# A spectral filter and a two-level expert layer on one core: a block-diagonal table for the forward transform, PSUM units whose two banks are no longer ordered, a third store buffer and a new written order

## The chip, the cores and the metric

The kernel runs on one core of one Trainium2 chip. The metric is the device time of one execution in microseconds, the median over several runs. The core has five engines that run side by side and meet at semaphores: TensorE (PE for its matmuls, PEld for its weight loads), VectorE (DVE), ScalarE (ACT), GpSimd (POOL) and SyncE (SP, which here only issues DMAs). Matmuls write PSUM, which has eight banks of 128 x 512 fp32; ACT and DVE read it.

## What is computed

x is 8 x 1856 x 256 in fp32. The first part is a filter over the 1856 positions of each of the eight sequences:

```
X  = rfft(x, axis=1)
Yr = Xr @ w_r - Xi @ w_i + b_r
Yi = Xr @ w_i + Xi @ w_r + b_i
Y  = soft_threshold(Yr, 0.01) + 1j * soft_threshold(Yi, 0.01)
y  = irfft(Y, n=1856, axis=1)
```

The second part sends each of the 14848 rows of y to one of 4 groups and, inside it, to one of 4 experts, by the largest of two sets of logits. The expert computes relu(row @ w1) @ w2 with 1024 hidden values, scaled by the two softmax weights of the choice. An expert's rows are known only when the rows before it have been routed.

## The kernel before

**Two parts.** The span falls into a part whose order is written out by hand (about its first 565 us) and a part that works through all experts (the rest). In the second part line 455 is the first matmul of an expert (up), lines 516 and 517 the second (down). The diff does not touch it. The first part does the transforms, the routing and some early expert work, so that TensorE has something to do while routing ends.

**The steps of the first part.** The sequences go through in four pairs. One letter of the string ORDER is one step, and PE, ACT, DVE and SP each execute their instructions in that order. POOL's queue is filled by the framework's scheduler, but a scatter is tied to the matmul of two PE steps before it. The letters:

- l: a load of x or of an expert's weights (SP). c, d: first stage of the forward transform, 64 x 64 matmuls (line 324, PE), then transposes into the tile zys (line 328, DVE).
- e: second stage, with the table T (line 584, PE). One e makes two frequencies k. f and h: ACT copies the result of one k as its high half (line 597), DVE subtracts to get the low half (line 602).
- j, k, n, m, o: ACT writes the bias into PSUM (line 607), PE does twelve 128 x 512 matmuls for the complex weights (line 616), ACT takes the positive and the negative relu (line 624, tiles rp and rn, two buffers each), DVE subtracts them into zys (line 630).
- r, s: first stage back (line 644, PE; transposes at line 652, DVE). v: second stage back (line 663, PE). w and x: ACT copies one half of the v result to a store buffer ysb (line 674; two buffers) and after both halves issues the store to ys_d (line 676); DVE transposes the same half into yt (line 682; five buffers).
- G, H, R, S: logits by 64 matmul instructions on four yt tiles (line 692), a transpose (line 701), some 33 small steps of routing for a half pair (lines 156 to 231, DVE and a little ACT and PE), and the scatter of one column of row numbers into the lists (line 240, POOL).
- W, V, I, Z, F, T, X, Y, U, A, B, D, E, J, K: early expert work for eight jobs: split of the weights into halves, lists, fetch of rows (line 422, POOL), transposes (line 762), the up matmuls (line 783), the relu and its low half (lines 791, 795), the down matmuls (lines 807, 809), the scaling (line 817, ACT), the sum (line 823, DVE) and the store (line 502, POOL). L and M read the final lists and fetch the first rows of the second part.

**PSUM in the first part.** The pool "pa" holds three units of two banks (`banks()`); c, e, r, v, G, the routing matmuls, T and D each take one, and a step that needs a fourth waits until the oldest has been read. Two more banks hold the k results. The framework orders every two accesses to one unit that come from different engines, in the order in which they are written. In e one k lies in 256 columns of both banks; in v and D the halves lie one in each bank.

**fp32.** An fp32 matmul of the source shows up in the trace as two loads and two matmul instructions (480 matmuls of e are 960 of line 584). The matmuls of e take 64 rows: zys keeps one sequence of the pair in partitions 0 to 63 and the other in 64 to 127, and T holds the same 64 x 64 table twice, one below the other, so that a matmul per half is issued.

Of the kernel before, what the change touches and what calls it, by code (L numbers as in the profile page):

```python
# [9 lines left out]
F32 = mybir.dt.float32  # L10
# [27 lines left out]
jejleffhlhkknmjofhcmncdjdfkddhokmnjocmncdjedddocffchhkddddkmnjocmncdjedddoeffhhkkmnjofhemfnhkjoefmhnejokkmfnhjokmfnhjokm  # L38
njofhemnjokfhkmfnhjokfnhmjormnjokssrmnjoesseffhhkrfmhnkjssorfmhnkjssovnmvxwxvwxwvxwxvjxkxxwwxowwGnmjowwvxHvwxwvxxcwRxwxc
xwdlwRdGRddRRRRRRcHcdcdldcddledddefRfRhhcRRcddklddRRRRkRfRRmhnRRRjRkfmhnojoRknmjoRenRmRRjReRffhRRSRkhRoRRSRRRRkRfRnSRmRh  # L40
joRkRfSRmhnRRRjRSRRkRmRRnSjooRRneRmSRefRRjRSReRfohhSkSkfnhSmjorSmfnhkjsSsSormfnhSkjssSormSnjoesSskfhSrmSfnhcjsSscSdvldvx
wwdSkxwwxxSdovmSnvxwxvwxwvSxwxGjoSwwwSwkxxxSHRvmRRSnvxwxcwxcwSxwdlGjdSddRRRRRcRReddRReHRffhhkRRRRRRRRRRkRmfonhjoRkmnjofR
hemRnRjRkRfRRhSRRRoRkmRSRfRRnRRhjSRkmRRnojoSRRReRmRRnRSRRjRReRffcShdlkhSdoRkmSfnhjoSRkmRnRRSjRRRcmRoSncdjdldSdoeSrffhShk
ssSrmSnjoksSsSrmnjoeSssefSfhhkSSrfmhnSkjssSovfnShvwxwvxwxvSwxmvxxjSkxwxwxwoSwvmnGSjowwSwwkHSxxxRSRvRnRRvwxwxexwwxIRGmRRf
RfRjRRhRZhkHRRRRRRRRkRmRRnjooRRneRmRjRReRffRhSRRkRhRSRRRSRRRRknRRfoRmRSRRjRRefhSmhnRRSRkRjRRooSRkfmShnSjoRkfRmRnRRjSRRem
hSnRokjoSfhkmSnoSmSnorFsSsrWSWVWVSWTsWWFsWWVrXVSYlVUSsUsSABrAVBVSUWsWSWsUWSAVvAVlBvwxwvxSwxvwxSxvxSxWxWxWBWVwSVwVGwSVwlV
# [72 lines left out]
def spectral_moe(ctx: ExitStack, tc: tile.TileContext, x, wri, bri, wgate, w1, w2, cst, out):  # L119
# [171 lines left out]
    T = cf.tile([128, K1, 64], F32, name="T")  # L291
# [885 lines left out]
```

## Time and profile before

| | |
|---|---|
| median of 3 runs | 1218.77 us (1211.72 to 1220.06) |
| profiled execution | 1220.21 us, of which the span from first to last instruction is 1218.4 us |
| PE busy | 1139.5 us, 94% |
| DVE, ACT, POOL busy | 664.1, 540.9 and 397.0 us |
| mean granted TensorE clock | 0.967 |
| instructions | 20694 |

The busy time of PE is a union of modelled matmul intervals, so two matmuls that overlap count once, and a busy PE is not PE at its peak. An idle time stands in brackets behind an instruction with the instruction that ended it. The granted clock is 1.0 or 0.5 at any moment; a figure between is a mean over a stretch.

### The profile page before, as it was taken

To read this page: it belongs to the slowest core of one execution; us is meant where nothing else is said; L and a number is where in the kernel's file an instruction comes from. 1 tells how busy PE (TensorE), PEld (TensorE's weight loads), DVE (VectorE), ACT (ScalarE), POOL (GpSimd) and SP (SyncE) were. 2 spreads that over 40 slices of the span, in tenths; PEclk is the share of its full clock that TensorE was granted. 3 is DMA by queue.
4 is the path that set the end of the run, shared out by engine and by line. 5 is a ranking of instruction groups with operands and counts; after the bars stand their busy time and mean duration, and the time that the engine had idled before them with its cause. 6 is when DMAs were issued, how large, how long until landed. Compare 5 with 4: busy or idle time off the path is not lost. (4 is left out here: it accounts for less than half of the span.)

```text
span 1218.4 us, 20694 instructions
## 1 busy us (share of the span) xinstructions
PE 1139.5 (94%) x7762; PEld 913.8 (75%) x7762; DVE 664.1 (55%) x1453; ACT 540.9 (44%) x1234; POOL 397.0 (33%) x450
## 2 busy tenths in 40 slices
PE   8999899799898767998999999999999999999996
PEld 5686586476675456887889888888888898788886
DVE  3535774676575745634565557346346564474452
ACT  2464364344445332422454446346345454363442
POOL 0000034314326334654233332332343333323321
PEclk8999999999899888998999999999999999999999
DMA  9400610412221543122143324434533354345300
GB/s 388 132 2 3 240 36 2 158 52 71 70 71 18 136 160 87 49 69 88 49 181 107 118 103 173 185 112 140 215 126 110 114 181 178 117 146 203 117 30 24
DMA packets 42360, 138.94 MB, mean 114 GB/s; under 512 B 17318, under 2 KB 19628, under 8 KB 31890
## 3 DMA queue, kind: packets, MB, share of 16 engines
q1 hardware_dynamic: 21458, 89.21, 21.2%
q0 software_dynamic: 15904, 31.48, 8.1%
q10 hardware_dynamic: 4896, 16.91, 3.7%
q8 instruction: 62, 1.02, 0.4%
q14 instruction: 40, 0.33, 0.1%
HBM read 103.49 MB, written 35.00 MB: 114 GB/s over the span
## 5 line engine op out<-in xcount | busy, mean ns | idle before, releaser
L516 PE MATMUL py<-big,hh 128*128 128x512 f32 x824 | 298.4, 402 | 0.0
L455 PE MATMUL ph<-xth,big 128*128 128x384 f32 (+1 forms) x896 | 257.8, 363 | 5.2 <-ACT xth L442 3.6
L240 POOL DMA_INDIRECT lst<-ent,sloti x128 | 132.2, 1033 | 335.7 <-DVE xl L602 189.6
L517 PE MATMUL py<-big,hl 128*128 128x256 f32 x824 | 231.6, 281 | 0.0
L461 DVE SCALAR_TENSOR_TENSOR hl<-ph,hh 128x256 fp32r<-128x256 f32 x448 | 151.0, 379 | 78.8 <-ACT hh L459 68.7
L455 PEld LDWEIGHTS ph<-xth,big 128*128 128x128 f32 x896 | 166.4, 189 | 25.1 <-ACT xth L442 3.8
L516 PEld LDWEIGHTS py<-big,hh 128*128 128x128 f32 x824 | 155.0, 188 | 37.4 <-issue 3.2
L459 ACT ACTIVATE hh<-ph 128x256 fp32r<-128x256 f32 x448 | 137.8, 371 | 85.2 <-PE ph L455 80.4
L455 PE MATMUL ph<-xtl,big 128*128 128x384 f32 (+1 forms) x448 | 162.4, 362 | 0.1
L502 POOL DMA_INDIRECT out_dram<-yo,si_f x96 | 97.7, 1018 | 183.7 <-DVE yo L524 159.3
L517 PEld LDWEIGHTS py<-big,hl 128*128 128x128 f32 x824 | 155.0, 188 | 0.1
L422 POOL DMA_INDIRECT xg<-ys_d,gi_f x96 | 93.5, 974 | 187.8 <-PE pg L438 164.1
L524 DVE SCALAR_TENSOR_TENSOR yo<-py,ent_f,yo 128x256 f32<-128x256 f32 x96 | 46.4, 483 | 163.3 <-ACT yo L523 122.5
L523 ACT ACTIVATE yo<-py,ent_f 128x256 f32<-128x256 f32 x96 | 45.6, 475 | 193.7 <-PE py L517 152.2
L405 DVE TENSOR_TENSOR big<-xt,big 128x512 fp32r<-128x512 f32 x160 | 108.8, 680 | 0.0
L404 ACT CAST big<-xt 128x512 fp32r<-128x512 f32 x160 | 104.0, 650 | 0.0
L616 PE MATMUL pw<-wh,xh 128*128 128x512 f32 x240 | 102.0, 425 | 0.0
L616 PE MATMUL pw<-wl,xh 128*128 128x512 f32 x240 | 97.6, 407 | 0.0
L455 PEld LDWEIGHTS ph<-xtl,big 128*128 128x128 f32 x448 | 84.9, 190 | 8.1 <-DVE xtl L443 0.5
L584 PEld LDWEIGHTS bank<-T,big 64*128 64x128 f32 x960 | 63.1, 205 | 15.7 <-issue 7.6
L584 PE MATMUL bank<-T,big 64*128 64x64 f32 x960 | 66.4, 293 | 4.6 <-DVE big L328 3.0
L624 ACT ACTIVATE rp<-pw,nlam 128x512 f32<-128x512 f32 x60 | 41.2, 687 | 65.7 <-PE pw L616 54.5
(187 smaller groups left out, 1629.1 us busy)
## 6 DMA issues: line engine op xcount, KB each, us to landing
xt<-in_w_dram SPq DMA_DIRECT2D x48, 1024.0 KB
ys_d<-ysb ACTq DMA_DIRECT2D x32, 512.0 KB
big<-in_w_dram SPq DMA_DIRECT2D x16, 1024.0 KB
big<-in_x_dram SPq DMA_DIRECT2D x8, 1024.0 KB
xt<-in_x_dram SPq DMA_DIRECT2D x8, 1024.0 KB
lst<-ent,sloti POOLq DMA_INDIRECT x128
lst<-zero SPq DMA_DIRECT2D x1, 1920.0 KB
xg<-ys_d,gi_f POOLq DMA_INDIRECT x96
```

What stands on the lines that cost most here:

```text
L240: ins = nc.gpsimd.indirect_dma_start(out=lst, out_offset=bass.IndirectOffsetOnAxis(ap=sl_, axis=0), in_=en_, in_offset=None, bounds_check= ...
L404: nc.scalar.copy(out=wt[:, 2 * i, cs], in_=raws[i][:, cs])
L405: nc.vector.tensor_tensor(out=wt[:, 2 * i + 1, cs], in0=raws[i][:, cs], in1=wt[:, 2 * i, cs].bitcast(F32), op=ALU.subtract)
L422: ins = nc.gpsimd.indirect_dma_start(out=xg[:, c, :], out_offset=None, in_=ys_d[0:rows, :], in_offset=bass.IndirectOffsetOnAxis(ap=ids.gi[ ...
L455: nc.tensor.matmul(o[:, :n], lhsT=a_[:, ch, fs], rhs=b_[:, ch, 0:n], start=k == 0, stop=k == 5)
L459: nc.scalar.activation(out=hh[:, f, :m], in_=ov, func=AF.Relu)
L461: nc.vector.scalar_tensor_tensor(out=hl[:, f, :m], in0=ov, scalar=0.0, in1=hh[:, f, :m].bitcast(F32), op0=ALU.max, op1=ALU.subtract)
L502: ins = nc.gpsimd.indirect_dma_start(out=out, out_offset=bass.IndirectOffsetOnAxis(ap=ids.si[:, t:t + 1], axis=0), in_=ysb, in_offset=None ...
L516: nc.tensor.matmul(o, lhsT=hh[:, f, ts], rhs=w2b[:, :, f, :], start=f == 0, stop=f == 7, skip_group_check=True)
L517: nc.tensor.matmul(o[:, 0:D], lhsT=hl[:, f, ts], rhs=w2h[:, f, :], start=False, stop=f == 7, skip_group_check=True)
L584: nc.tensor.matmul(ov, lhsT=zys[pr][rows_, k, bt, :, kp], rhs=T[rows_, 2 * k + kp, :], start=True, stop=True, skip_group_check=True)
L616: ins = nc.tensor.matmul(y, lhsT=a_[:, c * 128:c * 128 + 128], rhs=w_[:, c // 2, c % 2].rearrange("p j e -> p (j e)"), start=False, stop=a ...
```

## The change

- **The table.** T gets 128 columns per slot in place of 64 and is zeroed by POOL at the start. The raw table is loaded into a buffer of the pool "xt" (two buffers, which the loads of x and of weights use too), and POOL copies it into the two diagonal blocks, in three calls of two copies. A matmul of e then takes all 128 rows and writes 128 columns; the number of matmuls halves (240 in the source), and one k fills one bank in the order in which f and h want it.
- **Banks not ordered.** `apart` declares that f of one k and h of the other k of a unit, w of one half and x of the other half, and D of one half against E and J of the other have no dependency. w now takes the second half first while x takes the first.
- **Buffers.** ysb has three buffers (two before), yt four (five), rn one (two); rp has none, because the positive relu is written straight into zys and o subtracts rn there.
- **The order.** ORDER is another permutation of the same 1434 letters, each as often as before.

```diff
--- before.py
+++ after.py
...
@@ -288,7 +288,8 @@
     nc.scalar.dma_start(out=cA, in_=cst[:, _OFF["A"][0]:_OFF["A"][0] + 64])
     nc.scalar.dma_start(out=K, in_=cst[:, CK0:CK1])
     nc.vector.tensor_copy(out=base, in_=kc("EB"))
-    T = cf.tile([128, K1, 64], F32, name="T")
+    T = cf.tile([128, K1, 128], F32, name="T")
+    nc.gpsimd.memset(T, 0.0)
     wf = fwd.enter_context(tc.tile_pool(name="wf", bufs=2))
     pw = fwd.enter_context(tc.tile_pool(name="pw", bufs=2, space=PSUM))
 
@@ -344,8 +345,14 @@
         for bt in range(2):
             a_last = turn_a(0, i, bt, o[:, bt])
 
-    nc.sync.dma_start(out=T.rearrange("p k c -> p (k c)"), in_=cst[:, 0:CF1])
-    craw = wf.tile([128, 2 * D], F32, name="rn")[:, 0:128]
+    traw = xp.tile([128, K1, 64], F32, name="xt")
+    nc.sync.dma_start(out=traw.rearrange("p k c -> p (k c)"), in_=cst[:, 0:CF1])
+    def t_blocks(k):
+        for h in range(2):
+            nc.gpsimd.tensor_copy(out=T[64 * h:64 * h + 64, k].rearrange("p k (j h c) -> p k j h c", j=2, h=2)[:, :, :, h, :], in_=traw[64 * h:64 * h + 64, k, :].rearrange("p k (j c) -> p k j c", j=2))
+
+    t_blocks(slice(0, 6))
+    craw = wf.tile([128, 2 * D], F32, name="rn", bufs=1)[:, 0:128]
     nc.sync.dma_start(out=craw, in_=cst[:, CF1:CI0])
 
     wraw = xp.tile([128, 2, 2, D], F32, name="xt")
@@ -362,6 +369,8 @@
     for w_ in (wh, wl):
         nc.scalar.activation(out=w_[:, 1, :, 0], in_=w_[:, 0, :, 1].bitcast(F32), func=AF.Copy, scale=-1.0)
         nc.scalar.copy(out=w_[:, 1, :, 1], in_=w_[:, 0, :, 0].bitcast(F32))
+    t_blocks(slice(6, 18))
+    t_blocks(slice(18, 30))
     nc.scalar.copy(out=sl, in_=craw)
     nlam = cf.tile([128, 1], F32, name="nlam")
     nc.vector.memset(nlam, -LAM)
@@ -544,6 +553,11 @@
             return run()
         return wrap
 
+    def apart(ins, key, *others):
+        for o in others:
+            tc.declare_no_dep(ins.ins, group=str(o), reason="the two work in different banks")
+        tc.add_to_no_dep_group(str(key), ins.ins)
+
     def pop(key):
         return units.pop(key), low.pop(key)
 
@@ -573,33 +587,26 @@
 
     @steps_of(pairs, u8)
     def f_mm(pr, kk):
-        psum["f", pr, kk] = o = banks()
+        unit = banks()
         for k in range(2 * kk, min(2 * kk + 2, 15)):
+            psum["f", pr, k] = o = unit[:, k % 2]
             for kp in range(2):
                 for bt in range(2):
-                    c0 = k % 2 * 256 + (2 * kp + bt) * 32
-                    for h in range(2):
-                        rows_ = slice(64 * h, 64 * h + 64)
-                        ov = o[:, h, c0:c0 + 160].rearrange("p (j c) -> p j c", c=32)[:, 0:5:4]
-                        nc.tensor.matmul(ov, lhsT=zys[pr][rows_, k, bt, :, kp], rhs=T[rows_, 2 * k + kp, :], start=True, stop=True,
-                                         skip_group_check=True)
-
-    def f_view(pr, k):
-        o = psum["f", pr, k // 2][:, :, k % 2 * 256:k % 2 * 256 + 256]
-        return o.rearrange("p h (j c) -> p j h c", j=2)
-
-    def f_cols(t):
-        return t.rearrange("p (j h c) -> p j h c", j=2, h=2)
+                    m = 2 * kp + bt
+                    nc.tensor.matmul(o.rearrange("p (j c) -> p j c", j=4)[:, :, m * 32:m * 32 + 32],
+                                     lhsT=zys[pr][:, k, bt, :, kp], rhs=T[:, 2 * k + kp, :], start=True, stop=True,
+                                     skip_group_check=True)
 
     @steps_of(pairs, k15)
     def f_high(pr, k):
         units["f", pr, k] = xh = wf.tile([128, 512], F32R, name="xh")
-        nc.scalar.copy(out=f_cols(xh), in_=f_view(pr, k))
+        apart(nc.scalar.copy(out=xh, in_=psum["f", pr, k]), ("f", pr, k), ("h", pr, k ^ 1))
 
     @steps_of(pairs, k15)
     def f_low(pr, k):
         low["f", pr, k] = xl = wf.tile([128, 512], F32R, name="xl")
-        nc.vector.tensor_tensor(out=f_cols(xl), in0=f_view(pr, k), in1=f_cols(units["f", pr, k]).bitcast(F32), op=ALU.subtract)
+        apart(nc.vector.tensor_tensor(out=xl, in0=psum["f", pr, k], in1=units["f", pr, k].bitcast(F32), op=ALU.subtract),
+              ("h", pr, k), ("f", pr, k ^ 1))
 
     @steps_of(pairs, k15)
     def m_bias(pr, k):
@@ -609,6 +616,7 @@
     @steps_of(pairs, k15)
     def m_mm(pr, k):
         xh, xl = pop(("f", pr, k))
+        del psum["f", pr, k]
         y = psum["m", pr, k]
         for a_, ws in ((xh, (wh, wl)), (xl, (wh,))):
             for c in range(4):
@@ -620,14 +628,16 @@
     def m_relu(nm, store, sign):
         @steps_of(pairs, k15)
         def run(pr, k):
-            store[nm, pr, k] = t = wf.tile([128, 512], F32, name=nm)
+            t = z_of(pr)[:, k]
+            if sign < 0:
+                store[nm, pr, k] = t = wf.tile([128, 512], F32, name=nm, bufs=1)
             nc.scalar.activation(out=t, in_=psum["m", pr, k], func=AF.Relu, bias=nlam, scale=sign)
         return run
 
     @steps_of(pairs, k15)
     def m_sub(pr, k):
-        rp, rn = units.pop(("rp", pr, k)), low.pop(("rn", pr, k))
-        nc.vector.tensor_tensor(out=z_of(pr)[:, k], in0=rp, in1=rn, op=ALU.subtract)
+        z = z_of(pr)[:, k]
+        nc.vector.tensor_tensor(out=z, in0=z, in1=low.pop(("rn", pr, k)), op=ALU.subtract)
 
     def z_of(pr):
         return zys[pr].rearrange("p k b d q -> p k (b d q)")
@@ -667,20 +677,23 @@
     ysbs, yts, group = {}, {}, []
 
     @steps_of(pairs, u8, two)
-    def p_out(pr, v, h):
-        if h == 0:
-            ysbs[pr, v] = wi.tile([128, 4, D], F32, name="ysb", bufs=2)
+    def p_out(pr, v, i):
+        h = 1 - i
+        if i == 0:
+            ysbs[pr, v] = wi.tile([128, 4, D], F32, name="ysb", bufs=3)
         ysb = ysbs[pr, v]
-        nc.scalar.copy(out=ysb[:, :, h * 128:h * 128 + 128], in_=psum["p", pr, v][:, h].rearrange("p (s d) -> p s d", s=4))
-        if h == 1:
+        apart(nc.scalar.copy(out=ysb[:, :, h * 128:h * 128 + 128], in_=psum["p", pr, v][:, h].rearrange("p (s d) -> p s d", s=4)),
+              ("w", pr, v, h), ("x", pr, v, i))
+        if i == 1:
             nc.scalar.dma_start(out=y_v[pr, :, 4 * v:4 * v + 4, :], in_=ysb)
 
     @steps_of(pairs, u8, two)
     def p_turn(pr, v, h):
         if v % 2 == 0:
-            yts[pr, v // 2, h] = wi.tile([128, 4, 2, 4, 32], F32, name="yt", bufs=5)
-        nc.vector.transpose(out=yts[pr, v // 2, h][:, :, v % 2].rearrange("p c s n -> p s c n"),
-                            in_=psum["p", pr, v][:, h].rearrange("p (s d) -> p s d", s=4))
+            yts[pr, v // 2, h] = wi.tile([128, 4, 2, 4, 32], F32, name="yt", bufs=4)
+        apart(nc.vector.transpose(out=yts[pr, v // 2, h][:, :, v % 2].rearrange("p c s n -> p s c n"),
+                                  in_=psum["p", pr, v][:, h].rearrange("p (s d) -> p s d", s=4)),
+              ("x", pr, v, h), ("w", pr, v, 1 - h))
 
     @steps_of(pairs, range(2))
     def g_mm(pr, h):
@@ -804,24 +817,27 @@
         o, ts = psum["d", n, t], slice(t * 128, (t + 1) * 128)
         w2b, w2h = views(wts[jobs[n][1]])[2:]
         for f in range(half * 4, half * 4 + 4):
-            nc.tensor.matmul(o, lhsT=hid[n][0][:, f, ts], rhs=w2b[:, :, f, :], start=f == 0, stop=f == 7,
-                             skip_group_check=True)
+            first_ = nc.tensor.matmul(o, lhsT=hid[n][0][:, f, ts], rhs=w2b[:, :, f, :], start=f == 0, stop=f == 7,
+                                      skip_group_check=True)
             ins = nc.tensor.matmul(o[:, 0:D], lhsT=hid[n][1][:, f, ts], rhs=w2h[:, f, :], start=False, stop=f == 7,
                                    skip_group_check=True)
+            for i_ in (first_, ins):
+                apart(i_, ("D", n, t), ("E", n, 1 - t), ("J", n, 1 - t))
         pace[:] = pace[-1:] + [ins.ins.name]
 
     @steps_of(range(len(jobs)), range(2))
     def down_act(n, t):
         units["y", n, t] = ysb = yp[-1].tile([128, D], F32, name="yo")
         j, e = jobs[n]
-        nc.scalar.activation(out=ysb, in_=psum["d", n, t][:, D:], func=AF.Copy, scale=lev[j, e].ent[:, t, 1:2])
+        apart(nc.scalar.activation(out=ysb, in_=psum["d", n, t][:, D:], func=AF.Copy, scale=lev[j, e].ent[:, t, 1:2]),
+              ("E", n, t), ("D", n, 1 - t), ("J", n, 1 - t))
 
     @steps_of(range(len(jobs)), range(2))
     def down_add(n, t):
         j, e = jobs[n]
         ysb = units["y", n, t]
-        nc.vector.scalar_tensor_tensor(out=ysb, in0=psum.pop(("d", n, t))[:, 0:D], scalar=lev[j, e].ent[:, t, 1:2], in1=ysb,
-                                       op0=ALU.mult, op1=ALU.add)
+        apart(nc.vector.scalar_tensor_tensor(out=ysb, in0=psum.pop(("d", n, t))[:, 0:D], scalar=lev[j, e].ent[:, t, 1:2], in1=ysb,
+                                             op0=ALU.mult, op1=ALU.add), ("J", n, t), ("D", n, 1 - t), ("E", n, 1 - t))
 
     @steps_of(range(len(jobs)), range(2))
     def down_out(n, t):
```

The two orders differ nearly everywhere; the stretch from the last r to the last G of each, as an example (before, then after):

```
rAVBVSUWsWSWsUWSAVvAVlBvwxvwxSwxvwxSxvxSxWxWxWBWVwSVwVGwSVwlVSVVlwvwxHvSwxwDxSxxDwRRwTEDRXJRKYDRRRRIURERJURAKRRBRUARZRBRURARFRBDRARRBRvFRxWDWxWVRFDWRWRRWG
rAVBVUWsSWWsUSAWBvASVBDlwxxwTVvSXVYDwSxxwvSVWVWvxlwVwUxwSxWUxwSVWGVEVSAJAlBKBUSHRRSURARBSvRARBvwxxDwRRwRvxxwDxwIRwxDERRJRRvKRRRxDwZWxwRDRRFWRRRWDRWWVRFWRRG
```

## Rows read from the trace of the kernel before

**Rows 1.** The page: the granted clock in 40 equal slices of the span (9 is 90% or more).

```profile
PEclk8999999999899888998999999999999999999999
```

**Rows 2.** Sums by stretch: the stretch in us, its length, then the busy time and count of PE, PEld, DVE, ACT and POOL, the mean granted clock, the DMA share and GB/s.

```profile
0.00:568.00 568.00, 501.55 (x4206) 361.50 (x4207) 323.15 (x623) 234.88 (x421) 179.22 (x189) 0.93 0.30 98
568.00:1213.00 645.00, 637.99 (x3558) 552.29 (x3556) 341.00 (x830) 305.99 (x814) 217.83 (x261) 1.00 0.37 129
239.00:291.00 52.00, 47.62 (x384) 34.16 (x378) 38.77 (x92) 25.39 (x45) 15.45 (x15) 0.97 0.23 64
406.00:466.00 60.00, 41.50 (x390) 30.51 (x390) 35.01 (x72) 22.95 (x44) 21.28 (x25) 0.83 0.46 140
```

**Rows 3.** The waits of PE in the first 563 us: who waited for whom, us in total, how often, the longest.

```profile
PE bank L663 <- DVE yt L682: 10.3, 5, 5.5
PE bank L692 <- ACT ysb L674: 8.4, 4, 5.2
PE bank L208 <- DVE oh L202: 4.3, 1, 4.3
PE bank L807 <- DVE yo L823: 3.7, 4, 1.4
PE bank L663 <- ACT ysb L674: 3.7, 3, 1.5
PE bank L762 <- DVE L L701: 3.6, 1, 3.6
PE bank L324 <- ACT ysb L674: 3.2, 2, 1.7
```

**Rows 4.** The timeline of ACT in the last pair's v stage: start in us, length, what, and in brackets the idle time before it and what ended it. ACTq is ACT issuing the store.

```profile
409.98 0.59 ACT L674 COPY ysb<-bank 128x512 f32<-128x512 f32 x1 [0.50 <-PE bank L663]
411.35 0.59 ACT L674 COPY ysb<-bank 128x512 f32<-128x512 f32 x1 [0.78 <-DVE yt L682]
...
414.65 0.33 ACTq L676 DMA_DIRECT2D ys_d<-ysb  x1
...
421.81 0.33 ACTq L676 DMA_DIRECT2D ys_d<-ysb  x1
...
431.44 1.07 ACT L674 COPY ysb<-bank 128x512 f32<-128x512 f32 x2 [8.10 <-DMA ys_d<-ysb]
```

**Rows 5.** The timeline of DVE in the same place.

```profile
410.60 0.72 DVE L682 STREAM_TRANSPOSE yt<-bank 128x512 f32<-128x512 f32 x1 [0.45 <-ACT ysb L674]
411.97 0.72 DVE L682 STREAM_TRANSPOSE yt<-bank 128x512 f32<-128x512 f32 x1 [0.65 <-ACT ysb L674]
```

**Rows 6.** The timeline of PE in the first pair's v stage, and in the last pair's.

```profile
120.88 1.13 PE L663 MATMUL bank<-big,CI 64*64 64x256 f32 x16 [1.01 <-ACT ysb L674]
123.25 1.14 PE L663 MATMUL bank<-big,CI 64*64 64x256 f32 x16 [1.23 <-ACT ysb L674]
...
130.81 2.90 PE L663 MATMUL bank<-big,CI 64*64 64x256 f32 x48
...
421.84 5.03 PE L692 MATMUL bank<-yt,wg 64*64 64x256 f32 x64 [5.18 <-ACT ysb L674]
426.70 1.07 PE L663 MATMUL bank<-big,CI 64*64 64x256 f32 x16
433.31 1.99 PE L663 MATMUL bank<-big,CI 64*64 64x256 f32 x16 [5.54 <-DVE yt L682]
```

**Rows 7.** The timeline of PE around two consecutive e steps, around 64 instructions of G at full clock, and in the early up matmuls.

```profile
53.69 3.99 PE L584 MATMUL bank<-T,big 64*128 64x64 f32 x64
57.60 0.50 PE L616 MATMUL pw<-wh,xh 128*128 128x512 f32 x1
57.94 0.40 PE L616 MATMUL pw<-wl,xh 128*128 128x512 f32 x1
...
127.30 3.68 PE L692 MATMUL bank<-yt,wg 64*64 64x256 f32 x64
...
401.25 0.28 PE L783 MATMUL ph<-xtl,big 128*128 128x256 f32 x1
...
403.74 0.28 PE L783 MATMUL ph<-xth,big 128*128 128x256 f32 x1
```

**Rows 8.** Line 783 by itself: its weight loads, min, median and max ns, first and last start.

```profile
L783 PEld LDWEIGHTS ph<-xth,big x256: 186/188/337, 401.0 to 547.4; 128*128 128x128 f32 x128
```

**Rows 9.** The timeline of POOL: the first scatter of the last pair, two in the dense stretch, the last of all.

```profile
463.91 1.00 POOL L240 DMA_INDIRECT lst<-ent,sloti  x1 [10.24 <-issue]
...
513.95 0.97 POOL L240 DMA_INDIRECT lst<-ent,sloti  x1 [0.30 <-issue]
515.23 0.97 POOL L240 DMA_INDIRECT lst<-ent,sloti  x1 [0.30 <-issue]
...
537.58 0.97 POOL L240 DMA_INDIRECT lst<-ent,sloti  x1 [1.17 <-PE ph L783]
```

**Rows 10.** The head, three timelines together: POOL's zeroing of 256 columns and its subtraction of 1024 columns, ACT's cast of the small table that is loaded behind T on the same queue, PE's first e.

```profile
0.72 0.31 POOL L380 MEMSET zero<- 128x256 f32 x1 [0.29 <-POOLq L1165]
...
16.08 0.30 ACT L365 CAST sl<-rn 128x128 bf16<-128x128 f32 x1 [13.14 <-DMA rn<-in_cst_dram]
...
18.53 2.36 POOL L360 TENSOR_TENSOR wl<-xt,wh 128x1024 fp32r<-128x1024 f32 x1 [17.50 <-ACT wh L359]
...
18.02 7.26 PE L584 MATMUL bank<-T,big 64*128 64x64 f32 x64 [1.81 <-DVE big L328]
```

More of the change, by code (lines that the diff above doesn't have):

```diff
@@ L37 @@
 ORDER = """
[L38 to L46, printed above, removed]
@@ L47 @@
-SVVlwvwxHvSwxwDxSxxDwRRwTEDRXJRKYDRRRRIURERJURAKRRBRUARZRBRURARFRBDRARRBRvFRxWDWxWVRFDWRWRRWGRWRWRERSVwwJVSVDHlSRRTEVTKX
-JRYTSRRURRRSRURARSRBARBKURRRSRURARRRSBDARRXBSYDVFVUVEJlRUASBDASBUSUKABDSAXBSRYWRRWUSRWRWURFWRWRTRWVDWVESVDAJABSBUEVSJUVA
-VKBDAVSXBDYSVUESJUAKBDSABUSUSABDFABDEJSDSTEDXJSYTKUSUABSDABSUEJKUASBDAXSBDYKUEKJUAKBLDABDUEJMUABDABDDEJDKDEKJDKEJK
+jejleffhlhkkfnhmojefnhmcojcddkddcfnhcmdkdjddocfnhcmdcdjdcdkddddoemnojefhkkfnhmojefnhmeojkkfnhmojkfnhmojkfnhmojkfnhmojkfn
+hmojenmefojhekefnhmkojkfnhmjokfnhmojkfnhmojrfmhnksjsokfnhmojrnmjokssrnmojesseffhhkrfnhmksjsocfnhcmdcdjldcdvdldvxwxwvdwdc
@@ new lines @@
+xxwcdwdvdldcxxwcdwdvdldkxxwowGnmojvxxwkxwHwRxRvRnRRmvRxwRewxxwjxefRowhfGRhRRRRRRRkRRRRHRRRRkfnhmojRRfkRnhmRojRkRnRmRSojR
+RReRnRSRefRRmhRjRkSfoRRRShRRkRfRRnRhSmRojRrRmRSRnRjksSsoSRRmrRnRRjSoessSeffhRkRSRRhSrfmhnSksjsSorfnShmesjSscovSddkwxSxwv
+fSmhvwxnxkwSxwowxjSvfnhvwxmSvxwoGwjSSkHxSxwxwRvwxSRmvxwcwxSxwclwdkdRndSdjxRoScmRRnGRdljdSRRRoSRcRHRcdcdSldcddleddedfRfRh
+RkRRRRhRRRRkfnhmojRRfeRnRmRRjeRokRRShRRRRRkSRfRnRRmRoSjhefRnRhRSmRkRojRRRSRRRRRkRfnSmhojRSRfkRmhnRSjRRRkfRmhSRonejSomnrf
+oSjhksSsrSfnhmkSsjsSormnSojksSsrnSmojesSseffhShvvxwSxwkxwwxSvfmShvwxnxkwxSwowxjSGfmhnojSvHSvxwvxwxvwSRwxkxwxwSxwRRxwkRSR
@@ new lines @@
+mRRnRRojSRGmRnRRRjSRoRRReHRRRIeRfRRfRhRhkRZRRRRkfRmShnRRSRRojRkfRSRmhnRRojRkRmSRnRRSRjRRRRSemRRRRoeRfRfnShRRjhkSRRSRRRkf
+RRmhoSnSjomknSomSnoSrFssSrWWVWSVWsWSTWsXFWYWrVVVSlUsSUsASBrAVBVUWsSWWsUSAWBvASVBDlwxxwTVvSXVYDwSxxwvSVWVWvxlwVwUxwSxWUxw
+SVWGVEVSAJAlBKBUSHRRSURARBSvRARBvwxxDwRRwRvxxwDxwIRwxDERRJRRvKRRRxDwZWxwRDRRFWRRRWDRWWVRFWRRGWRWREREFRRJRJTHXSRTYRUVSRRR
+RUSRARRBFTARUBRRUVRASRBDARRSXBYDSRRRRRDFERRRUJVSRUAVlBSUVABSVUAVFBlDAXBRYWSRDWRWSRWDRERSWRRDWJKVWVWDVSVUVSVUVASVEBTKAUJB
+SDASBUSEJXTKAYBUSDSABDSEJKUSUABSDABSUEJKTXDASYBUSDSABUKEJUSABSDABSUKDAXBSDYEJSUKUAKBDAKBLUEJKUABDABMDDEJDDEJDKEKJK
```

## The prediction

> **What bounds the kernel now.** First the sums by stretch, with the clock's slices beside them [rows 1, 2]. In the second part PE is busy 637.99 of 645 us at clock 1.00; the change does not touch it and I leave its time alone. In the first 568 us PE is busy 501.55 us, so 66 us are idle, and the mean clock is 0.93. As the clock is either full or half, 0.07 x 568 = 40 us of full-speed work is lost to it on top. Some 106 us are thus to be had at most, and never all of it. The slices show where: one half-speed slice at the head, then the low digits between about 400 and 490 us. Next the waits of PE in that part [rows 3]: the largest end with the two readers of the v units, ACT's copy to ysb and DVE's transpose to yt. The timelines of ACT and DVE [rows 4, 5] show why. The copy of the first half starts at 409.98, its transpose at 410.60, the copy of the second half at 411.35, its transpose at 411.97: four reads in single file, also the second copy after the first transpose, which read different banks. And on ACT a copy waits 8.10 us for a store to land before a buffer is free.
>
> **The change, term by term** (savings in us; the ends go into the range).
>
> *e.* 64 instructions took 57.60 - 53.69 = 3.91 us [rows 7], 61 ns each; 960 of them 58.7 us. Afterwards there are 480 with twice the columns. 64 instructions of G, four at a time on quarters of the array and 256 columns each, took 3.68 us, so 128 fp32 columns stream in 3.68 / 16 / 2 = 0.115 us. The early up matmuls have full-array loads and nearly the same stream: 22 steps from 401.25 to 403.74, 113 ns each [rows 7], although a load takes 188 ns [rows 8]; there the load hides under the matmul before. I take 113 ns: 480 x 0.113 = 54.2, a saving of **4.5**. The best end is 4.5; the other is the second rival.
>
> *Tiling.* The first k matmul behind e takes 0.50 us where the next takes 0.40 [rows 7], 0.10 us for a change of array shape. Counted in the two orders, neighbouring PE steps differ in shape 92 times before and 78 times after (e now being full-array, like k): 14 x 0.10 = **1.4**, ends 0 and 3.
>
> *f, h, relu, o.* Same count and shape of reads; no row of PE's waits names f or h, so a shorter wait between them is hidden by the twelve k matmuls: **0**. If that cover is gone, k waits on the chain f, h.
>
> *Reads of v in pairs.* PE's waits on ysb and yt are 10.3 + 8.4 + 3.7 + 3.2 = 25.6 us [rows 3]. Two of them, 5.18 and 5.54 [rows 6], go back to a store; 14.9 are left. When units follow each other PE starts one every 123.25 - 120.88 = 2.37 us, where unhindered it needs 2.90 / 3 = 0.97 [rows 6]: 1.40 of stall. Reads two by two are bounded by two transposes, 1.44 us [rows 5], so 0.47 of stall remains, and two thirds of 14.9 go: **10**. Ends 0 (the two engines stay in single file for another reason) and 14.9. Late next: DVE, whose two transposes then set the pace.
>
> *Third store buffer.* The copy at 431.44 got the buffer whose store was issued at 421.81, 9.6 us earlier [rows 4]. With three it would wait for the one of 414.65, which at 9.6 us lands at 424.3; PE ended that unit at 426.70 + 1.07 = 427.8 [rows 6]. So at least 3.6 of the 5.54 go. Of 10.7 I take half, **5**; ends 3.6 and 10.7. Behind the waiting copy ACT also held the early experts' relus, which gain too.
>
> *D.* The second half's matmuls wait 3.7 us for the first half's sum [rows 3]; **3**, ends 0 and 3.7.
>
> *Clock.* 406 to 466 us has clock 0.83 and 239 to 291 has 0.97 [rows 2]: 60 x 0.17 + 52 x 0.03 = 11.8 us lost in the stretches of those stalls. 60% of the stalls (15 of 25.6) go, so 60% of this: **7**, ends 0 and 11.8.
>
> *The order.* The remaining named waits, on routing and its transpose, are 4.3 + 3.6 us [rows 3]. v steps stood in 11 runs of up to five and now in 18 of up to four, with k, U or D between, which is what idle time needs; but the mix of steps by stage is the same. I take **4**; ends -11 (the nearest rows for a badly placed step are the waits of 5.18 and 5.54 us [rows 6], both once more) and 8.
>
> *Head.* T arrives before the small table behind it on its queue, so by 16.08, and PE starts e at 18.02 because of a transpose [rows 10]. POOL's two first copies, 384 columns on 64 partitions, cost at its subtraction's 2.36 us per 1024 columns 0.9 us each: ready at 17.9. Cover 0.1 us; I charge **-1**, end -3. The zeroing, 15 x 0.31 = 4.7 us from 0.7 on, lies under the x loads; the later copies lie under e and k. The raw table takes the buffer into which the first x load of pair two went; it is needed only behind the first v stage, 100 us later [rows 6], but if SP holds it in front of pair one's rows, c starts late. I charge 0.
>
> *Fewer yt, rn and rp.* In the new order every G has exactly eight transposes of its pair before it per half (four tiles), and no n stands before the o that frees rn. ACT has j and f between, o is done under them: **0**, end -2.
>
> *POOL.* From 463.91 to 538.55 it issues the last 32 scatters, with some 16 fetches and stores between, 1.28 us apart in the dense stretch [rows 9]: 48 x 1.28 = 61 of 75 us. The chain moves forward with the last G, since scatters follow routing, but it has only 13 us of slack and 47 such steps remain: **-2**, end -5.
>
> Sum: 4.5 + 1.4 + 10 + 5 + 3 + 7 + 4 - 1 - 2 = **32 us**. The profiled execution took 1220.2 us (span 1218.4), 1.4 above the median; 1220.2 - 32 = 1188, and 1187 against the median.
>
> **Rivals.**
>
> *Given back at the end.* PE gets its v and G done earlier, but the lists are complete only with the last scatter, and POOL or DVE's routing steps take what PE saved. For it: 61 of 75 us on POOL, and scatters tied to PE steps. Against: the first scatter of the last pair found POOL idle for 10.24 us [rows 9], so the chain's start follows PE. Only e, tiling and some 4 us of the early pairs' stalls would stay, 10 in all: 1187 + 22 = **1209**.
>
> *Loads no longer hidden.* Full-array matmuls of e may have to wait for their load, as the two 64-row halves, which loaded past each other, did not: 0.188 + 0.115 = 0.303 x 480 = 145 us in place of 58.7, 87 more, so 1187 + 4.5 + 87 = **1278**. It decides from 180 ns per instruction, where the 27.5 us of the other terms are used up (58.7 + 27.5 = 480 x 0.180). Against it stand the 113 ns of the up matmuls, which are full-array with one load each. The Trainium skill, "TensorE: Matmul & The Clock Gate", Part 3, says that a load overlaps a running matmul only when their row groups differ; by that rule this rival comes true. The trace of the up matmuls disagrees: same row group, 188 ns loads, 113 ns steps.
>
> *Not what it says.* With w and x in fixed queues, ACT and DVE could go on in single file for another reason. Then the 10, the 3 and 6 of the clock's 7 fall away, 13 us remain, and the time is 1187 + 19 = **1206**.
>
> **Chances.** 0.68 for the forecast (1165 to 1206), 0.15 for the first rival, 0.07 for the third, 0.10 for slower, half of it unhidden loads and half an order that puts a step in a wrong place. About 1%, 12 us, is what a measurement can tell from no change: 1206.6 and 1231.0 are the borders. The first and third rival lie around the upper one's near side, so faster 0.72, same 0.18, slower 0.10. Range: the sum's upper ends (4.5 + 3 + 14.9 + 10.7 + 3.7 + 11.8 + 8 = 57) give 1162, the rivals reach 1209 with a few us more: 1164 to 1214.
>
> **What would show it.** Line 584 480 times with 113 ns between; in the v stage copy and transpose starting together and then again together; PE's waits on ysb and yt at 10 us or less; no wait of several us on a store; the stretch around 400 to 470 us with fewer half-speed windows; the first matmul of line 455 some 32 us earlier, and the second part as long as before. Wrong it would be with that matmul less than 12 us earlier and POOL busy without gaps before it, or with 200 ns and more between the matmuls of e.

## The result, and the profile after

| | before | after |
|---|---|---|
| median of 4 runs each | 1215.24 us (1211.15 to 1220.06) | 1179.33 us (1171.03 to 1180.85) |
| ratio | | 0.9689, interval 0.9625 to 0.9753 |
| profiled execution, span | 1220.21, 1218.4 us | 1180.85, 1179.0 us |
| PE busy | 1139.5 us | 1123.8 us |
| instructions | 20694 | 19743 |

The forecast was 1187, the sum of terms 32 us; 36 came by the medians and 39 in the two profiled executions. The medians, ratios and savings below leave out two executions in a slower state, 1395.12 us of before_apart and 1607.83 us of the kernel before. First the clock in 40 slices of the changed kernel, which answers to [rows 1].

```profile
PEclk9999999989998989899999999999999999999999
```

The 8 at the head is gone, and single low slices are left where a row of them stood. Then the sums by stretch, cut at the first matmul of line 464 (455 before), with which the second part begins: first of the kernel before, cut in the same way, which [rows 2] don't show, then of the changed one.

```profile
0.00:563.00 563.00, 496.79 (x4192) 357.14 (x4192) 321.23 (x617) 234.09 (x418) 176.06 (x185) 0.94 0.30 98
563.00:1218.00 655.00, 642.75 (x3570) 556.65 (x3570) 342.92 (x837) 306.78 (x817) 220.98 (x265) 0.99 0.37 128
```

```profile
0.00:524.00 524.00, 481.56 (x3713) 350.12 (x3713) 321.87 (x617) 235.86 (x418) 179.68 (x190) 0.96 0.33 104
524.00:1179.00 655.00, 642.28 (x3570) 556.25 (x3570) 342.84 (x837) 306.60 (x816) 222.91 (x268) 0.99 0.37 129
374.00:425.00 51.00, 47.79 (x480) 33.14 (x464) 39.53 (x78) 24.84 (x47) 20.28 (x22) 0.96 0.61 177
425.00:507.00 82.00, 66.26 (x411) 58.99 (x410) 38.37 (x79) 22.78 (x44) 51.19 (x54) 0.88 0.23 57
```

The second part is 655 us in both, so all 39 us come out of the first. There PE's idle time fell from 563 - 496.8 = 66.2 to 524 - 481.6 = 42.4 us, and its busy time by 15.2 us. The work of the others is the same: DVE, ACT and POOL are busy within 4 us of what they were. The last two rows are the last pair's v stage, now at clock 0.96, and what follows its last G, at 0.88. The waits of PE in the first part, which answer to [rows 3]:

```profile
PE bank L325 <- DMA xt<-in_x_dram: 6.1, 2, 5.9
PE ph L796 <- issue: 4.5, 2, 3.7
PE bank L820 <- ACT hh L804: 4.0, 1, 4.0
...
PE bank L705 <- DVE yt L694: 2.0, 1, 2.0
...
PE bank L820 <- DVE yo L839: 0.6, 1, 0.6
```

The readers of v, 25.6 us before, head the list no more: the waits on ysb (line 685) and yt (694) that PE has left come to 2.7 us, 2.0 of them in the row of line 705. At the top stands a wait that was not there, for a load of x. ACT's timeline in the last pair's v stage, and then DVE's, which answer to [rows 4, 5]:

```profile
385.37 0.59 ACT L685 COPY ysb<-bank 128x512 f32<-128x512 f32 x1 [1.15 <-PE bank L673]
386.12 0.59 ACT L685 COPY ysb<-bank 128x512 f32<-128x512 f32 x1 [0.17 <-DVE yt L694]
...
397.37 0.59 ACT L685 COPY ysb<-bank 128x512 f32<-128x512 f32 x1 [4.50 <-DMA ys_d<-ysb]
```

```profile
385.37 1.33 DVE L694 STREAM_TRANSPOSE yt<-bank 128x512 f32<-128x512 f32 x2 [0.42 <-PE bank L673]
```

Copy and transpose both start at 385.37, and the second copy follows at 386.12, while DVE is in its second transpose: a unit is read in 1.34 us, where the four reads in single file took from 409.98 to 411.97 + 0.72, or 2.71 us. A wait for a store is still there, 4.50 us where it was 8.10.

### The profile page after: what moved, and what is told of

Its sections match the earlier page's. It is cut to its first block, busy times and chain, and to the rows that moved or that the text cites. A ratio compares the mean times of both kernels' runs of the same rounds, so it can differ in the third digit from the quotient of the medians.

```text
span 1179.0 us, 19743 instructions
## 1 busy us (share of the span) xinstructions
PE 1123.8 (95%) x7282; PEld 906.4 (77%) x7282; DVE 664.7 (56%) x1453; ACT 542.5 (46%) x1234; POOL 402.6 (34%) x457
## 5 line engine op out<-in xcount | busy, mean ns | idle before, releaser
L240 POOL DMA_INDIRECT lst<-ent,sloti x128 | 129.8, 1014 | 298.0 <-DVE sloti L227 147.0
L525 PEld LDWEIGHTS py<-big,hh 128*128 128x128 f32 x824 | 155.0, 188 | 37.5 <-issue 3.2
L624 PE MATMUL pw<-wh,xh 128*128 128x512 f32 x240 | 98.4, 410 | 2.7 <-ACT pw L614 2.1
L624 PE MATMUL pw<-wl,xh 128*128 128x512 f32 x240 | 95.1, 396 | 0.5 <-POOL wl L367 0.5
L603 ACT CAST xh<-bank 128x512 fp32r<-128x512 f32 x60 | 34.5, 587 | 75.4 <-PE pw L624 47.2
L608 DVE TENSOR_TENSOR xl<-bank,xh 128x512 fp32r<-128x512 f32 x60 | 41.2, 694 | 48.7 <-PE pw L624 28.2
L596 PEld LDWEIGHTS bank<-T,big 128*128 128x128 f32 x480 | 59.9, 199 | 10.4 <-issue 5.0
```

What stands on the lines that cost most here:

```text
L240: ins = nc.gpsimd.indirect_dma_start(out=lst, out_offset=bass.IndirectOffsetOnAxis(ap=sl_, axis=0), in_=en_, in_offset=None, bounds_check= ...
L525: nc.tensor.matmul(o, lhsT=hh[:, f, ts], rhs=w2b[:, :, f, :], start=f == 0, stop=f == 7, skip_group_check=True)
L596: nc.tensor.matmul(o.rearrange("p (j c) -> p j c", j=4)[:, :, m * 32:m * 32 + 32], lhsT=zys[pr][:, k, bt, :, kp], rhs=T[:, 2 * k + kp, :], ...
L624: ins = nc.tensor.matmul(y, lhsT=a_[:, c * 128:c * 128 + 128], rhs=w_[:, c // 2, c % 2].rearrange("p j e -> p (j e)"), start=False, stop=a ...
```

## The experiments

The chips differ: the kernel before takes 1186.5 us on both chips of the first eight runs and 1215.3 on that of the last four; in the comparison above it took 1215.2. So ratios are compared, and microseconds only where the kernel before takes the same time. The table has every run; a saving is the kernel before less the kernel of the row.

| run | median us | ratio, interval | saving |
|---|---|---|---|
| after_again (no edit) | 1155.98 | 0.9735, 0.9701 to 0.9768 | 30.5 |
| before_again (no edit) | 1187.14 | 0.9998, 0.9971 to 1.0025 | -0.6 |
| after_old_order | 1161.71 | 0.9792, 0.9766 to 0.9817 | 24.8 |
| after_ordered | 1165.84 | 0.9827, 0.9805 to 0.9849 | 20.7 |
| after_two_stores | 1159.93 | 0.9790, 0.9756 to 0.9825 | 26.6 |
| after_old_table | 1163.80 | 0.9817, 0.9780 to 0.9855 | 22.7 |
| before_new_order | 1172.04 | 0.9891, 0.9845 to 0.9937 | 14.5 |
| before_apart | 1172.96 | 0.9890, 0.9846 to 0.9933 | 13.5 |
| after_third (no edit) | 1177.29 | 0.9684, 0.9645 to 0.9723 | 38.0 |
| after_old_order_ordered | 1210.21 | 0.9966, 0.9945 to 0.9987 | 5.1 |
| after_x_early | 1173.03 | 0.9656, 0.9627 to 0.9686 | 42.3 |
| after_no_early_stores | 1165.00 | 0.9585, 0.9545 to 0.9625 | 50.3 |

### Both kernels once more

> The changed kernel unaltered, beside the next three on one chip. The four runs before fell on a chip on which the kernel before takes 1186.5 us in place of 1215. If the chips differ by a constant ratio: 0.969 times the kernel before. If what the change saves is partly a cost that only the slower chip has: 0.975 to 0.98 here.

> The kernel before unaltered, for its trace on the same chip: ratio 1.00. The traces of the two kernels on one chip tell which waits and half-speed stretches belong to the kernel and which to the chip.

Both without an edit. The gain is there on another chip, 30.5 us. The ratio, 0.9735, lies between the two that were expected; its interval leaves out 0.969 and just takes in 0.975, so part of the gain may belong to the slower chip, but the interval of the comparison above (0.9625 to 0.9753) overlaps, so this stays open. In the kernel before, the stalls of the v stage head PE's list on this chip too:

```profile
PE bank L663 <- DVE yt L682: 12.2, 5, 7.2
PE bank L692 <- ACT ysb L674: 7.6, 4, 4.0
...
PE bank L663 <- ACT ysb L674: 4.3, 3, 2.0
```

### One part taken out of the changed kernel

```diff
# after_old_order: the string of the kernel before
-jejleffhlhkkfnhmojefnhmcojcddkddcfnhcmdkdjddocfnhcmdcdjdcdkddddoemnojefhkkfnhmojefnhmeojkkfnhmojkfnhmojkfnhmojkfnhmojkfn
+jejleffhlhkknmjofhcmncdjdfkddhokmnjocmncdjedddocffchhkddddkmnjocmncdjedddoeffhhkkmnjofhemfnhkjoefmhnejokkmfnhjokmfnhjokm
...
# after_ordered: nothing is declared
     def apart(ins, key, *others):
-        for o in others:
-            tc.declare_no_dep(ins.ins, group=str(o), reason="the two work in different banks")
-        tc.add_to_no_dep_group(str(key), ins.ins)
+        return
# after_two_stores
-            ysbs[pr, v] = wi.tile([128, 4, D], F32, name="ysb", bufs=3)
+            ysbs[pr, v] = wi.tile([128, 4, D], F32, name="ysb", bufs=2)
# after_old_table: T, its load, e, f and h as before
-    T = cf.tile([128, K1, 128], F32, name="T")
-    nc.gpsimd.memset(T, 0.0)
+    T = cf.tile([128, K1, 64], F32, name="T")
...
```

> The changed kernel with the written order of before (all else changed). Theory (the parts of the code save the time, reads two by two and the third store buffer above all; the order adds some 4 us): 1181 to 1190 us. Rival (the new order saves most): 1198 us or more, with PE waits on ysb and yt back above 15 us.

> The changed kernel without the declarations, so that accesses to the two banks of a unit are ordered again. Theory: it loses the 10 us of reads two by two, the 3 us of the down step and part of the clock term, 1190 to 1200 us, with the four reads of a v unit in single file. Rival: the new order already spaces the v steps, so that little waits on them: under 1184 us.

> The changed kernel with two store buffers. Theory: 5 to 10 us more, 1183 to 1190 us, with waits of ACT on stores of several us in the last pair's v stage. Rival (the new order alone keeps stores and copies apart): within 3 us of the changed kernel.

> The changed kernel with the 64-row table and its 960 matmul instructions (f and h of different k ordered again, since they share banks). Theory: 3 to 6 us more from the matmuls and changes of array shape, 1181 to 1185 us; if the half-speed stretch of 10 us at the head of the kernel before comes from the 64-row matmuls, it is back and costs 5 us more. Rival: the table does more than its matmul time, because a k waits for f and h of both banks: 1190 us or more.

Against after_again's 1155.98 the declarations are worth 9.9 us as the last part put in, the table 7.8, the order 5.7 and the third buffer 4.0. For the first two the intervals of the ratios lie apart from after_again's; that of the order touches it, and that of the buffer overlaps, so the buffer's 4 us are not told from nothing. By their ratios, order and declarations cost about what the theory said; the buffer cost less than the 5 to 10 us expected, although ACT's waits for stores in the first part are 20.3 us in after_two_stores and 5.4 in after_again. The table's 7.8 us are more than its matmuls (3 to 6), and the half-speed stretch at the head is back in part; the rival, that k waits for f and h of both banks, was not told from this. What the declarations do is seen in after_ordered, on ACT and then on DVE:

```profile
406.92 0.59 ACT L683 COPY ysb<-bank 128x512 f32<-128x512 f32 x1 [0.50 <-PE bank L671]
408.89 0.59 ACT L683 COPY ysb<-bank 128x512 f32<-128x512 f32 x1 [1.38 <-DVE yt L692]
```

```profile
407.54 1.31 DVE L692 STREAM_TRANSPOSE yt<-bank 128x512 f32<-128x512 f32 x2 [0.39 <-ACT ysb L683]
```

With the new string, but ordered banks, copy, two transposes and copy stand one behind the other again, 2.56 us a unit.

### One part put into the kernel before

```diff
# before_new_order: the string of the changed kernel
-jejleffhlhkknmjofhcmncdjdfkddhokmnjocmncdjedddocffchhkddddkmnjocmncdjedddoeffhhkkmnjofhemfnhkjoefmhnejokkmfnhjokmfnhjokm
+jejleffhlhkkfnhmojefnhmcojcddkddcfnhcmdkdjddocfnhcmdcdjdcdkddddoemnojefhkkfnhmojefnhmeojkkfnhmojkfnhmojkfnhmojkfnhmojkfn
...
# before_apart: apart() as in the changed kernel, for w and x and for D, E and J; w takes the second half first
-    def p_out(pr, v, h):
-        if h == 0:
+    def p_out(pr, v, i):
+        h = 1 - i
+        if i == 0:
...
+        apart(nc.scalar.copy(out=ysb[:, :, h * 128:h * 128 + 128], in_=psum["p", pr, v][:, h].rearrange("p (s d) -> p s d", s=4)),
+              ("w", pr, v, h), ("x", pr, v, i))
...
# after_old_order_ordered: both first edits of the section above, so that table and buffers alone are new
```

> The kernel before with the new written order alone. Theory (the parts of the code save most): ratio 0.995 to 1.005, because the four reads of a v unit stay in single file. Rival (the order saves most): 0.975 to 0.985.

> The kernel before with only the declarations for copy and transpose of v (and the other half first in the copy) and for the down step, old order, old buffers, old table. Theory (reads two by two are the largest part): ratio 0.985 to 0.99. Rival (in the old order the two queues stay in step anyway, so it needs the new order too): 0.997 to 1.003.

> The new table and the new buffers alone: old order, banks ordered. Theory (table 8 us and store buffer 4 us, by what each lost when taken out): ratio 0.988 to 0.992. Rival (they gain only where the reads go two by two): 0.996 or more.

Order alone 14.5 us, declarations alone 13.5 (by the ratios some 13 us each, so neither is the larger), table and buffers alone 5.1 of 1215.3, on the other chip. For the order neither expectation came: theory and rival lie on either side of 0.9891. The declarations did what was expected of them. For table and buffers the theory missed and the rival came, ratio 0.9966.

The first two overlap, as either shortens the same stalls: PE's waits on the two readers of v, 26.6 us in all rows of before_again, are 13.0 in before_new_order and 18.2 in before_apart. Two rows lead the latter:

```profile
PE bank L668 <- DVE yt L689: 9.3, 5, 5.7
PE bank L700 <- ACT ysb L680: 6.8, 2, 5.6
```

ACT's waits for stores are what they were there, 19.4 us for 19.5, as before_apart keeps two buffers. By the medians the order alone is worth two and a half times what it is worth as the last part (14.5 and 5.7). PE's waits in before_new_order show how it does that without a declaration:

```profile
PE pg L438 <- DMA xg<-ys_d,gi_f: 5.0, 1, 5.0
PE bank L324 <- DMA xt<-in_x_dram: 4.5, 1, 4.5
PE bank L692 <- DVE yt L682: 3.7, 2, 3.3
PE bank L663 <- ACT ysb L674: 3.5, 4, 1.6
```

In before_new_order the units of v stand apart with other steps between, and two rows with 7.2 us are left near the top for the readers of v. In exchange there is a 4.5 us wait for x, which before_again does not list among its largest: the new string makes it.

Part of the 5.1 is seen at the head: the window from 12 to 32 us, and the same step of the first k in it, of the kernel before and then of after_old_order_ordered.

```profile
12.00:32.00 20.00, 17.68 (x118) 12.94 (x111) 8.55 (x14) 7.73 (x15) 2.36 (x1) 0.74 1.02 420
28.75 1.09 PE L616 MATMUL pw<-wh,xl 128*128 128x512 f32 x4
```

```profile
12.00:32.00 20.00, 17.32 (x110) 10.53 (x103) 11.24 (x19) 10.50 (x19) 6.70 (x7) 1.00 1.01 405
24.97 1.09 PE L622 MATMUL pw<-wh,xl 128*128 128x512 f32 x4
```

The clock is 1.00 in place of 0.74, and the same step comes 3.8 us earlier. These two executions are 11.3 us apart, though, where the medians are 5.1 apart, and a kernel with the new table can also have 0.91 at its head (last section). So the head is a part of the gain, and how the rest divides between table and buffers is not shown.

### What is left to gain

> The changed kernel unaltered, beside the three above on one chip: ratio 0.970 to 0.977, as in the last comparison.

after_third is the changed kernel on the chip of these runs, with 1177.29 us; its ratio, 0.9684, lies just below the expected 0.970 to 0.977, which its interval takes in.

```diff
# after_x_early: the last pair's second c, two d and the load behind it some 60 letters earlier
-RReRnRSRefRRmhRjRkSfoRRRShRRkRfRRnRhSmRojRrRmRSRnRjksSsoSRRmrRnRRjSoessSeffhRkRSRRhSrfmhnSksjsSorfnShmesjSscovSddkwxSxwv
-fSmhvwxnxkwSxwowxjSvfnhvwxmSvxwoGwjSSkHxSxwxwRvwxSRmvxwcwxSxwclwdkdRndSdjxRoScmRRnGRdljdSRRRoSRcRHRcdcdSldcddleddedfRfRh
+RReRnRSRefRRmhRjRkSfoRRRShRRkRfRRnRhSmRojRrRmRSRnRjksSsoSRRmrRnRRjSoessSeffhRkRSRRhSrfmhnSksjsSorfnShmesjSscovSddkcwxSxw
+ddlvfSmhvwxnxkwSxwowxjSvfnhvwxmSvxwoGwjSSkHxSxwxwRvwxSRmvxwcwxSxwclwdkdRndSdjxRoSmRRnGRjSRRRoSRcRHRcdcdSldcddleddedfRfRh
# after_no_early_stores: the first 12 of the 16 stores of early expert rows are not issued
-        store(units.pop(("y", n, t)), lev[j, e], t, "out")
+        if 2 * n + t < 12:
+            units.pop(("y", n, t))
+            return
+        store(units.pop(("y", n, t)), lev[j, e], t, "out")
```

> The changed kernel with the written order altered in one place: the second c of the last pair (and its two d) some 60 letters earlier, so that an input buffer is free earlier, and the third and fourth x load of that pair right behind the c that frees theirs. In the changed kernel PE waits 5.4 us for the last x load at 241 us, and the clock is at half speed for 6.8 us behind it. Theory (that wait is new with the order and on the path): 5 to 9 us less than the changed kernel, 0.967 to 0.970 of the kernel before where the changed one had 0.9735. Rival (POOL's scatters at the end take the time back): within 2 us of the changed kernel.

> The changed kernel without the first 12 of the 16 stores of the early expert jobs, so the rows of those jobs are missing from the output; all else is issued. Theory (after the change POOL's queue, 1.28 us per issue, sets the end of the first part): some nine stores before the last scatter go, the last scatter comes 8 to 12 us earlier after the last G, PE's wait for the first gather shrinks from 7.9 us to under 2 us, and the time is 7 to 10 us less than the changed kernel's. Rival (the end is set by PE and the landing of DMAs): within 3 us.

after_no_early_stores leaves out those stores and with them the rows that they write. **The x load.** c waits for it in after_third, and hardly in after_x_early:

```profile
243.38 3.46 PE L325 MATMUL bank<-xt,cA 64*64 64x512 f32 x16 [6.11 <-DMA xt<-in_x_dram]
246.77 3.45 PE L596 MATMUL bank<-T,big 128*128 128x128 f32 x27
```

```profile
239.62 1.95 PE L325 MATMUL bank<-xt,cA 64*64 64x512 f32 x16 [0.84 <-DMA xt<-in_x_dram]
```

The wait cost twice: the 16 matmuls behind it took 3.46 us where they take 1.95, as the clock fell while PE stood (0.79 from 236 to 252 us, 1.00 in after_x_early). At the end of the third pair's v, 319.6 us in after_third, after_x_early stands at 314.3, and 4.3 of these 5.3 us are seen between the medians, less than the 5 to 9 expected. The intervals of the two ratios overlap, so the median's gain is not told from nothing; the wait and the clock behind it are shown by the traces. With one and the same string the wait also varies: it is 6.4 us in after_third and 2.8 in after_no_early_stores.

**POOL's queue.** From the last G on, the ends of the steps and the start of part two stand so in the traces (us):

| | last G | last scatter | first matmul of part two | last G to part two |
|---|---|---|---|---|
| before | 466.1 | 538.5 | 563.1 | 97.0 |
| after | 424.6 | 506.3 | 524.0 | 99.4 |
| after_third | 422.6 | 504.6 | 522.4 | 99.8 |
| after_no_early_stores | 419.1 | 490.2 | 508.4 | 89.3 |

The last G came 41.5 us earlier with the change, the last scatter 32.2: the chain of scatters kept 9.3 us of it, and as the way from there to part two became 6.9 us shorter, 2.4 were lost on balance. Without the 12 stores the last scatter comes 14.4 us earlier and part two 10.5 us sooner behind the last G, and the median falls by 1177.29 - 1165.00 = 12.3 us, although only POOL and its DMAs have less to do. 3.5 us of the trace's 14.0 come ahead of the last G, with a shorter wait for x, 2.8 us in place of 6.4; that wait is over some 160 us before the first store that is left out, so the 10.5 are what the stores explain. 7 to 10 had been expected, and under 3 by the rival, which fell.

So what stands in POOL's queue has a part in the end of the first part. That POOL alone sets it is not shown: on this chip POOL also waits for PE, as a scatter is tied to a matmul. These are POOL's waits in after_third from the last G on, and the sums from the last G to the last scatter, of after_third and of after_no_early_stores:

```profile
POOL lst L240 <- PE ph L796: 9.2, 5, 3.0
POOL lst L240 <- PE bank L822: 4.4, 3, 2.9
```

```profile
423.00:505.00 82.00, 66.34 (x413) 59.05 (x413) 38.78 (x79) 23.31 (x44) 50.66 (x55) 0.85 0.22 58
419.00:490.00 71.00, 62.01 (x405) 55.66 (x402) 38.94 (x81) 23.08 (x44) 41.33 (x44) 0.93 0.21 49
```

PE's idle time falls from 15.7 to 9.0 us with the stores gone, and its clock rises from 0.85 to 0.93, so PE's own stalls are part of the 10.5 us; by what way the stores cause them was not followed. Whether POOL had this part before the change was not tried. How full its queue can be shows best in after_again, on PE at the seam and on POOL before it:

```profile
492.00 0.28 PE L822 MATMUL bank<-big,hl 128*128 128x256 f32 x1
500.21 1.72 PE L447 MATMUL pg<-K,xg 128*128 128x128 f32 x6 [7.93 <-DMA xg<-ys_d,gi_f]
```

```profile
485.22 0.98 POOL L240 DMA_INDIRECT lst<-ent,sloti  x1 [0.30 <-issue]
486.50 0.98 POOL L240 DMA_INDIRECT lst<-ent,sloti  x1 [0.30 <-issue]
487.79 0.98 POOL L511 DMA_INDIRECT out_dram<-yo,si_b  x1 [0.30 <-DVE yo L839]
489.07 0.98 POOL L511 DMA_INDIRECT out_dram<-yo,si_b  x1 [0.30 <-issue]
494.20 0.28 POOL L860 CAST gi_f<-ent_f 128x112 int32<-128x112 f32 x1 [4.15 <-DMA ent_f<-lst]
495.11 1.00 POOL L431 DMA_INDIRECT xg<-ys_d,gi_f  x1 [0.63 <-POOL gi_f L860]
```

An indirect DMA every 1.28 us, scatters and stores in one queue, then the list's way back, the first fetch, and PE 7.93 us idle for it. On the other chip this wait is not in after_third's list; there the early expert's own waits (lines 796 and 820) stand in its place.

## Why the prediction was right, point by point

The sum was 32 us, and 30.5, 38.0 and 35.9 us came, by chip and comparison; of its two kinds of terms both nearly came. The idle terms (10 + 5 + 3 + 4 - 1 - 2) made 19, and PE's idle time fell by 23.8; e, tiling and the clock made 12.9, and the busy time fell by 15.2. The mechanism was right, but that the sum came so near is in part luck, since the single terms were off by more: e and tiling were priced some 3 us too high and the clock some 5 too low. The range was also a little narrower than its working: it starts at 1164 where the upper ends of the sum give 1162.

- **Reads of v in pairs (10), third buffer (5).** The mechanism came as told, and PE's waits on the two readers went from 25.6 to 2.7 us, below the bound of 10. But declarations and order take the same waits: alone the two were worth 13.5 and 14.5, as the last part 9.9 and 5.7, so no single price of this term can be read off; both together without table and third buffer were not run. The third buffer came to 4.0 within its uncertainty, and a store is still waited for, 4.50 us, though the text had none of several us left; ACT bears it, and no row of PE's names it.
- **e (4.5).** 113 ns were taken. The timeline of PE after, around one e:

```profile
47.11 3.92 PE L596 MATMUL bank<-T,big 128*128 128x128 f32 x32
50.79 0.48 PE L624 MATMUL pw<-wh,xh 128*128 128x512 f32 x1
51.11 0.39 PE L624 MATMUL pw<-wl,xh 128*128 128x512 f32 x1
51.34 0.39 PE L624 MATMUL pw<-wh,xh 128*128 128x512 f32 x1
```

  From 47.11 to 50.79 it is 3.68 / 32 = 115 ns. In the median over all e at full clock it is 118 ns, and 62 in the kernel before: 960 x 0.062 = 59.5 less 480 x 0.118 = 56.6, a saving of 2.9 us. The rival of unhidden loads fell clearly; it decided from 180 ns. The loads take about as long as before, and are hidden:

```profile
L596 PEld LDWEIGHTS bank<-T,big x480: 193/196/331, 18.1 to 346.9; 128*128 128x128 f32 x160
```

  196 ns of load under steps of 115 is possible only where a load runs beside the matmul before it. The rule of the Trainium skill, "TensorE: Matmul & The Clock Gate", Part 3 (Packing small matmuls), that it does so only when the row groups differ, would have made 480 steps of some 0.3 us; in this trace the loads of one and the same row group overlap. That part of the Trainium skill also names a second case, a load into the background weight buffer, which the prediction left out; the steps of 115 ns do not contradict it.
- **Tiling (1.4).** The reason was wrong. The first k matmul behind e still takes 0.48 us, the next 0.39, though e and k have the same array shape now. So the 0.10 us of [rows 7] are not the price of a change of shape, and the term has nothing to stand on.
- **Clock (7).** Half-speed stretches up to the first matmul of part two, counted from the trace's clock records, were 70.3 us in all and are 37.5, so 18.7 us of full-speed work are lost in place of 35.2. Not all of it falls on a busy PE. With e's 2.9 the clock has to make about 12 of the 15.2 us of busy time; that is what is left over, not a measurement of its own. I had priced only the v stages and left out the head, where 0.26 of 20 us, 5.2, were lost: the first e with the next k behind it ran at half speed there; its 64 instructions took 7.26 us [rows 10], and 32 take 4.31 now:

```profile
18.10 4.31 PE L596 MATMUL bank<-T,big 128*128 128x128 f32 x32 [1.90 <-DVE big L329]
...
23.15 0.50 PE L624 MATMUL pw<-wl,xh 128*128 128x512 f32 x1 [0.51 <-POOL wl L367]
```

- **Head (-1).** e starts at 18.10 in place of 18.02, and one k waits 0.51 us for POOL's subtraction, since all six copies, not two, stand before it: 0.6 us. The gain from the clock in the same place was not in the sum.
- **D (3).** The wait of 3.7 us for the sum fell to 0.6, as predicted (line 820). D waits 4.0 us for ACT's relu there, where it was 2.8.
- **f, h, relu, o and fewer buffers (0).** No row of PE's waits after the change names f, h or rn, and the longest wait for o's result is 2.2 us where it was 2.1.
- **Order (4).** 5.7 as the last part (its interval touches that of no change), 14.5 alone: the size depends on what the declarations have already taken. Its price in a wrong place, which I had bounded by 11, came as well: 5.9 us for a load of x and the half-speed stretch behind it, of which the run with the earlier load had 4.3 back by the medians, within the noise.
- **POOL (-2), and the first rival.** Part two follows the last G by 99.4 us where it was 97.0: -2.4, near the term, though by another way than told, since the scatters kept 9.3 and what stands behind them gave 6.9 back. The rival (1209), in which POOL takes what PE saved, is thus false of this change; a part of its mechanism is there, as the missing stores show.
- **Third rival.** Copy and transpose start together, so it fell. after_ordered, where the single file is back, still saves 20.7 us; the rival would have left 13.

The second part stayed at 655 us, as said. Open is why the chips differ by 2.4% with one kernel, and how much of the clock's 12 us belongs to which part of the change.

## What to carry to other kernels

Price stalls and the clock together: here a stall of 6.1 us was paid again in matmuls that ran at half speed behind it, so a removed wait was worth more than its row. Before adding up parts that attack the same wait, ask what each is worth with the others in place; here two parts that take 14.5 and 13.5 us alone were worth 5.7 and 9.9 as the last. And when the engine at the bound gets faster, count the issues in the queues that run beside it (here 1.28 us for each indirect DMA, in after_again without a gap in the last 10 us before the lists are read) rather than read their share of busy time, which was 34% over POOL's span.

## What had not been expected of the hardware

At the head the clock went with the form of the work behind the stall. Where the first e runs in 64-row matmuls, the window from 12 to 32 us has clock 0.74 in the traces of before, before_again, before_new_order and before_apart, and 0.83 in after_old_table; in the nine traces where it runs in full-array ones, it is 0.91 or 1.00, though PE idles the same 1.8 to 1.9 us before it. With one and the same kernel it was 0.91 in after_again and 1.00 in the profile of the result and in after_third, so the form is not all of it, and the cause is not shown.

On the chip where all takes 2.4% longer, ACT and DVE have idle time in the first part that ended with nothing that the profile shows, as these two of the waits in after_third. In after_again neither engine has any such wait there, but in before_again DVE has one, of 3.3 us. What it is was not found.

```profile
DVE hl L808 <- issue: 9.2, 4, 3.5
ACT hh L804 <- issue: 8.2, 6, 2.3
```
